# Gathered rows turned by VectorE instead of TensorE, and small transfers moved from GpSimd's queue to SyncE's, in an attention and mixture-of-depths kernel

## The chip, the core and the metric

The kernel runs on one core of a Trainium2 chip. The metric is device time in microseconds (us) of one execution; a lower time is better. Engines are named as in the profile: PE is TensorE (PEld its weight loads), DVE is VectorE, ACT is ScalarE, POOL is GpSimd, SP is SyncE, which here only issues DMA transfers.

## What is computed

Eight sequences of 448 tokens pass through sigmoid attention with 12 heads of 64, and the result is the input x (448 x 768 per sequence) of a layer that sends only 128 tokens of each sequence through a feed-forward network. Everything is float32.

```python
scores = scale * np.matmul(q, k.transpose(0, 1, 3, 2)) - np.log(S)
attn = 1.0 / (1.0 + np.exp(-scores))
x = np.matmul(attn, v)                   # then (B,H,S,D) -> (B, S, H*D)
...
scores = np.einsum('bsd,d->bs', x, w_gate)
out = x.copy()
for b in range(B):
    top_idx = np.argpartition(-scores[b], capacity)[:capacity]   # 128 of 448
    xe = x[b, top_idx]
    h = np.maximum(xe @ w1, 0.0)         # 768 -> 1024
    ye = h @ w2                          # 1024 -> 768
    g = 1.0 / (1.0 + np.exp(-scores[b, top_idx]))
    out[b, top_idx] = x[b, top_idx] + g[:, None] * ye
```

## The kernel before

**Stages and units.** Four heads of one sequence form a group; a sequence has three groups, b has groups 3b to 3b+2. A stage s (0 to 11) works on two groups, 2s and 2s+1, in seven units n = 0 to 6. `unit(s, n)` (L197) makes 32 matmuls of scores (L213) into two PSUM tiles and two sigmoids on ACT (L221). After each unit `gap(s, n)` (L471) puts other work on the queues. The second matmul, attention times v, is `values(s, n)` (L224, matmuls L248): its part 0 stands at (s, 6), its parts 1 to 3 at (s+1, 0) to (s+1, 2). "(s, n)" below means the gap after unit n of stage s. Stage 12 has gaps only; after it a tail finishes the last sequences.

**Order.** The order is written out by hand: `manual_schedule` keeps the order of the program on every engine, and each engine and each DMA queue takes its own instructions strictly in that order. Tiles come from pools; an instruction that writes a buffer of a pool waits until the last reader of its former content is done.

**PSUM.** Two score tiles ("psc") and two tiles o0 and o1, each of two banks. `values` accumulates into o0 and o1; when its part 3 is done, `take` (L257) has VectorE copy them, transposed in 32 x 32 blocks, to x_b in SBUF: four instructions at L263, the first two empty o0, the others o1. Only then can o0 take the feed-forward's first group of the stage at (s, 3).

**Choosing the tokens of sequence b**, over about three stages, s being 2, 3, 5, 6, 8, 9, 11, 12 for b = 0 to 7:

- (s, 2), (s, 3): `gate_part` (L267; L271, L274), then `gate` (L285) on VectorE sums the gate score of each token; a DMA on POOL's queue writes them to DRAM (scores, L298).
- (s, 4): `store` (L276) writes x_b to DRAM in four DMAs of 2688 rows of 128 bytes (L280, SP's queue); `spread` (L307) brings the scores back to all 128 partitions (rep, L310, POOL's queue); for b = 1 it stands at (3, 6).
- (s+1, 1): `ranking` (L450): eight VectorE operations over 448 scores (L318, L321) count for each token how many are above it; `place` (L325) writes the ranks to DRAM and reads them back to all partitions (ranks L331, spot L333, both on POOL's queue). This stands on VectorE ahead of the stage's four L263.
- (s+1, 4): `copy_out` (L282) copies x from the DRAM buffer to the output (SP's queue).
- (s+2, 0), for b = 0 at (3, 6): `choose` (L455), `select` (L338): VectorE turns ranks into 128 row numbers and gates; POOL's indirect DMA gathers those rows (xe, L361).
- (s+2, 3): `follow` (L459): `turn_rows` (L366) transposes the 128 x 768 rows by six TensorE instructions (L375) into PSUM, ACT copies them to xeT (L381), and six groups of the feed-forward are put in a list: three `ffn1` (L384; 36, 36 and 24 matmuls, L391), three `ffn2` (L396; 16 matmuls, L401, then VectorE's L403).

At (s, 3), (s, 4) and (s, 5) `go` (L423) takes one group from the list, and at (s, 5) of stages 0 to 7 a second one while the list has more than one (L481). After stage 12 the tail (L522 to L540) does the rest: the last group of sequence 4, all of 5, 6 and 7, with `choose(6)`, `ranking(7)`, `copy_out(7)` and `choose(7)` between them. After each sequence's last ffn2 (for b = 7 after every one) an indirect DMA on POOL's queue writes the finished rows to the output (L408). It waits for the copies to the output that stand before it.

**SP's queue** holds all loads: k and q of group 2s+3 at (s, 1) and of 2s+4 at (s, 5) (L95), v for stage s+1 at (s, 0) (eight DMAs, L114 and L116, which wait until `values` is done with the buffer, at the end of (s, 2)), the weights, `store` and `copy_out`.

Of the kernel before, what the change touches and what calls it, by code (L numbers as in the profile page):

```python
# [17 lines left out]
def kernel(  # L18
# [11 lines left out]
    nc = tc.nc  # L30
# [15 lines left out]
    KD = D // P  # L46
    KF = F // P
    ND = D // 3
    SLOTS = [(s, min(P, CAP - s)) for s in range(0, CAP, P)]

    NC = -(-TB // 4)
    HELD = [TT * len(range(c, TB, NC)) for c in range(NC)]
# [1 line left out]
    NEG_LOG_S = -math.log(S)  # L54
    PSUM = bass.MemoryType.PSUM
    assert Dh == 2 * TT and TB == HK + 2 and S == TT * TB and H == 4 * NG and NQ == 2 * NS
    assert D == KD * P and F == KF * P and KF % 4 == 0 and 0 < CAP < S and D == HP * P


    const = ctx.enter_context(tc.tile_pool(name="const", bufs=1))  # L60
# [76 lines left out]
    earlier = const.tile([P, NC, S], mybir.dt.uint8, name="earlier")  # L137

    number = const.tile([P, TB, TT], mybir.dt.int16, name="number")
    slots = {s0: const.tile([P, 1], F32, name=f"slot{s0}") for s0, _ in SLOTS}  # L140
    score = const.tile([P, NC], F32, name="score")
    above = const.tile([P, NC], F32, name="above")
    level = const.tile([P, NC], F32, name="level")
# [3 lines left out]
    def constants():  # L147
        make_identity(nc, iden)
        for a in range(4):
            p = slice(a * TT, (a + 1) * TT)  # L150
            nc.gpsimd.dma_start(
                out=wg_b[p],
                in_=bass.AP(tensor=moe_w_gate.tensor, offset=moe_w_gate.offset + a * TT,
                            ap=[[0, TT], [P, HP], [1, TT]]))
        for s0, slot in slots.items():
            nc.gpsimd.iota(slot, pattern=[[0, 1]], base=s0, channel_multiplier=1,
                           allow_small_or_imprecise_dtypes=True)

        nc.gpsimd.memset(above, float(S))
        nc.gpsimd.memset(level, 0.0)  # L160
        for t in (score, gate_s, place_s):
            nc.gpsimd.memset(t, 0.0)
        mine = moe.tile([P, NC], F32, name="place")
        for a in range(4):
            nc.gpsimd.iota(mine[a * TT:(a + 1) * TT], pattern=[[1, NC]], base=a * NC,
                           channel_multiplier=TB, allow_small_or_imprecise_dtypes=True)
        every = moe.tile([P, TB, TT], F32, name="rep", bufs=2)
        nc.gpsimd.iota(every, pattern=[[1, TB], [TB, TT]], base=0, channel_multiplier=0,
                       allow_small_or_imprecise_dtypes=True)
        nc.gpsimd.tensor_copy(number, every)  # L170
        for c in range(NC):
            nc.gpsimd.tensor_scalar(
                out=earlier[:, c, :], in0=every.rearrange("p r t -> p (r t)"),
                scalar1=mine[:, c:c + 1], scalar2=None, op0=ALU.is_lt)
# [107 lines left out]
    def copy_out(b):  # L282
        nc.sync.dma_start(out=out[b], in_=st[b]["x_d"])

    def gate(b):  # L285


        nc.vector.tensor_reduce(out=gate_s[:, :TB], in_=gate_parts[b], axis=AX.X, op=ALU.add)
        by_dim = moe.tile([P, TT], F32, name="by_dim")
        nc.vector.transpose(by_dim, gate_s)  # L290
        parts = moe.tile([TT, 4, TT], F32, name="parts")
        for a in range(4):
            nc.vector.tensor_copy(parts[:, a], by_dim[a * TT:(a + 1) * TT])
        total = moe.tile([TT, TT], F32, name="total")
        nc.vector.tensor_reduce(out=total, in_=parts.rearrange("p a t -> p t a"), axis=AX.X,
                                op=ALU.add)
        scores = dram.tile([TB, TT], F32, name="scores")
        nc.gpsimd.dma_start(out=scores, in_=total[:TB])  # L298
        by_token = moe.tile([TT, TT], F32, name="by_token")
        nc.vector.transpose(by_token, total)  # L300
        for m in range(4):
            n = min(NC, TB - m * NC)
            nc.vector.tensor_copy(score[m * TT:(m + 1) * TT, :n],
                                  by_token[:, m * NC:m * NC + n])
        st[b]["scores"] = scores

    def spread(b):  # L307
        scores = st[b]["scores"]
        rep = st[b]["rep"] = moe.tile([P, S], F32, name="rep", bufs=2)
        nc.gpsimd.dma_start(out=rep, in_=bass.AP(tensor=scores.tensor, offset=scores.offset,  # L310
                                                 ap=[[0, P], [1, S]]))

    def rank(b, c):
        rep = st[b]["rep"]
# [10 lines left out]
    def place(b):  # L325

        nc.vector.tensor_add(place_s[:, :NC], above, level)
        by_col = moe.tile([P, TT], F32, name="by_col")
        nc.vector.transpose(by_col, place_s)
        ranks = dram.tile([P, TT], F32, name="ranks")  # L330
        nc.gpsimd.dma_start(out=ranks, in_=by_col)  # L331
        spot = moe.tile([P, 4, NC * TT], F32, name="spot")
        nc.gpsimd.dma_start(  # L333
            out=spot, in_=bass.AP(tensor=ranks.tensor, offset=ranks.offset,
                                  ap=[[0, P], [TT * TT, 4], [1, NC * TT]]))
        st[b]["spot"] = spot.rearrange("p m c -> p (m c)")[:, :S]

    def select(b, s0, n):  # L338

        picked = []  # L340
        for what in (number.rearrange("p r t -> p (r t)"), st[b]["rep"]):
            got = moe.tile([P, 1], F32, name="got", bufs=4)
            junk = moe.tile([P, S], F32, name="scr")
            nc.vector.scalar_tensor_tensor(
                out=junk[:n], in0=st[b]["spot"][:n], scalar=slots[s0][:n], in1=what[:n],
                op0=ALU.is_equal, op1=ALU.mult, accum_out=got[:n, 0:1])
            picked.append(got)
        row = moe.tile([P, 1], I32, name="row", bufs=2)
# [14 lines left out]
            in_offset=bass.IndirectOffsetOnAxis(ap=row[:n, 0:1], axis=0))  # L363
        st[b].update(idx=idx, gate=gt, xe=xe)

    def turn_rows(b, n, where="o"):  # L366
        if b == B - 3:
            lent = attnp.tile([P, 2, S], F32, name="attn0", bufs=NU + 3)
            xeT = lent[:, :, :KD // 2 * P].rearrange("p a (k n) -> p a k n", n=P)
        else:  # L370
            xeT = moe.tile([P, 2, KD // 2, P], F32, name="xeT")
        ps = banks(where).rearrange("p a (k n) -> p a k n", n=P)
        for t in range(KD):
            a, i = divmod(t, KD // 2)
            nc.tensor.transpose(ps[:, a, i, :n], st[b]["xe"][:n, t * P:(t + 1) * P],  # L375
                                iden[:n, :n])
        if where == "any":
            nc.scalar.activation(xeT[:, 0, :, :n], ps[:, 0, :KD // 2, :n], AF.Copy)
            nc.vector.tensor_copy(xeT[:, 1, :, :n], ps[:, 1, :KD // 2, :n])
        else:  # L380
            nc.scalar.activation(xeT[:, :, :, :n], ps[:, :, :KD // 2, :n], AF.Copy)  # L381
        st[b]["xeT"] = xeT

    def ffn1(b, n, f0, f1, where):  # L384
        xeT = st[b]["xeT"]
        if f0 == 0:
            st[b]["hT"] = moe.tile([P, KF, P], F32, name="hT")
        ps = banks(where)[:, 0].rearrange("p (k n) -> p k n", n=P)
        for f in range(f0, f1):
            for t in range(KD):  # L390
                nc.tensor.matmul(ps[:, f - f0, :n], w1_sb[:, t, f * P:(f + 1) * P],  # L391
                                 xeT[:, t // (KD // 2), t % (KD // 2), :n],
                                 start=(t == 0), stop=(t == KD - 1))
        nc.scalar.activation(st[b]["hT"][:, f0:f1, :n], ps[:, :f1 - f0, :n], AF.Relu)  # L394

    def ffn2(b, n, part, where):  # L396
# [26 lines left out]
    def go(where="o"):  # L423
        if ready:
            fn, args = ready.pop(0)
            fn(*args, where)

    late = {}

    def put(where, s, n, fn, *args):  # L430
        where.setdefault((s, n), []).append((fn, args))
# [5 lines left out]
    def routed(b):  # L437

        s = (NG * b + NG - 1) // 2 + 1
        put(late, s, 4, store, b)  # L440
        put(late, s, 4 if b != 1 else 6, spread, b)
        if s == NS:
            return
        put(late, s + 1, 1, ranking, b)
        put(late, s + 1, 4, copy_out, b)
        if s + 2 <= NS:
            put(late, *((s + 1, 6) if b == 0 else (s + 2, 0)), choose, b)
            put(late, s + 2, 3, follow, b)

    def ranking(b):  # L450
        for c in range(NC):
            rank(b, c)
        place(b)

    def choose(b):  # L455
        for s0, n in SLOTS:
            select(b, s0, n)

    def follow(b, where="o"):  # L459
        for s0, n in SLOTS:  # L460
            turn_rows(b, n, where)
            routed_groups(b, n)

    def gates(i):
        gate_part(i)
# [5 lines left out]
    def gap(s, n):  # L471
# [5 lines left out]
        if 3 <= n < NU - 1:  # L477
            if not ready:
                due(late, s, n)
            go("any" if s == NS else "o")  # L480
            if n == NU - 2 and s < NS - 4 and len(ready) > 1:  # L481
                go()
        if n == NU - 1 and s < NS:
            values(s, 0)
        due(late, s, n)
        if n == 3 and s > 0:
            if waiting:
                gate(waiting.pop())
# [4 lines left out]
    def stream():  # L493
# [35 lines left out]
        copy_out(B - 1)  # L529
        while len(ready) > 1:  # L530
            go("any")
        follow(B - 2, "any")
        for n in range(2):
            go("any")
        choose(B - 1)
        while len(ready) > 1:
            go("any")
        follow(B - 1, "any")
        while ready:
            go("any")  # L540
        assert not late
# [32 lines left out]
```

## Time and profile before

| what | value |
|---|---|
| median of 3 runs (lowest, highest) | 475.2 us (473.3, 479.42) |
| the profiled execution's own time | 476.17 us |
| its span in the profile | 474.4 us |
| mean granted TensorE clock | 0.991 |
| score matmuls into psc, L213 | 2496 x 542 ns each, 153.9 us busy |
| attention times v, L248 into o | 2304 x 540 ns with raw_v, 384 x 536 ns with raw_h |
| transposes of gathered rows, L375 | 48 x about 273 ns |
| copies of them by ACT, L381 | 6 x 0.81 us |

The profile is that of one execution. The busy time of an engine is the time in which it has at least one instruction under way; matmuls overlap each other, so the mean of one is longer than its share of the time. The chain of waits follows the work that ended last backwards and so gives the pieces that follow each other without overlap. The timeline gives each engine's instructions with their start, and in brackets how long the engine stood idle before and what it waited for. "SPq" is SP's DMA queue: the duration of an issue there is the time that the issuing took, not the time of the transfer. The DMA view gives the time from an issue to its landing.

### The profile page before, as it was taken

What the parts mean: (1) busy time and instruction counts of PE and PEld (TensorE: products, weight loads), DVE (VectorE), ACT (ScalarE), POOL (GpSimd) and SP (SyncE); (2) the same over time, 40 slices, a digit from 0 to 9 for tenths busy, and PEclk for the clock granted to TensorE, in tenths of its full rate; (3) what the DMA queues carried; (4) which work ended last, traced back from release to release, by engine and by line L of the source; (5) the groups of instructions that cost most, each with busy time, mean ns of one, the idle gap of its engine ahead of it and who ended that gap; (6) DMA issues with size and microseconds to landing.
All of it is one profiled execution on the core that took longest, in us unless ns stands there. A gap on an engine that the chain in (4) does not pass through costs nothing.

```text
span 474.4 us, 14579 instructions
## 1 busy us (share of the span) xinstructions
PE 457.4 (96%) x6582; PEld 312.6 (66%) x6582; DVE 227.3 (48%) x559; ACT 184.9 (39%) x245; POOL 48.8 (10%) x76
## 2 busy tenths in 40 slices
PE   8998989897999999999999999999999999999994
PEld 3563635365765684658774666755678738999993
DVE  4309087749140825765710864946254618530100
ACT  4756464544235334435445334445344420101000
POOL 9000000110000011011100011011010010220001
PEclk9999999999899999999999999999999999999999
DMA  8988788799921980985940992985822734722000
GB/s 268 229 324 212 291 196 178 158 262 195 227 70 45 202 202 8 229 177 149 258 171 3 202 202 43 266 153 130 254 69 43 155 83 79 209 57 68 35 0 33
DMA packets 119005, 72.74 MB, mean 153 GB/s; under 512 B 96320, under 2 KB 108800, under 8 KB 118688
## 3 DMA queue, kind: packets, MB, share of 16 engines
q1 hardware_dynamic: 115808, 61.35, 50.8%
q0 software_dynamic: 3136, 10.47, 10.0%
q8 instruction: 51, 0.84, 0.7%
q14 instruction: 10, 0.08, 0.0%
HBM read 57.51 MB, written 25.31 MB: 175 GB/s over the span
## 4 chain that ended last, share of the span: by engine, by line
PE 89%; DMA 4%; DVE 2%; ACT 1%; issue 1%; SPq 0%; POOLq 0%; DVEq 0%; ACTq 0%
PE o L248 25%; PE psc L213 24%; PE o L391 16%; PE o L401 13%; PE psc L401 4%; PE psc L391 3%; PE o L213 2%; DMA raw_h<-in_v_dram 1%; ACT attn L221 1%; DMA scores<-total 1%; DMA rep<-scores 1%; PE o L375 1%; PE o L506 1%; DVE scr L321 1%; DVE scr L318 1%
## 5 line engine op out<-in xcount | busy, mean ns | idle before, releaser
L221 ACT ACTIVATE attn<-psc,bias_s 128x896 f32<-128x896 f32 x156 | 148.6, 1004 | 121.0 <-PE psc L213 120.8
L213 PE MATMUL psc<-qT,kT 32*64 32x448 f32 x2496 | 153.9, 542 | 4.2 <-ACT attn L221 4.2
L248 PE MATMUL o<-attn,raw_v 32*64 32x448 f32 x2304 | 142.2, 540 | 1.1 <-ACT o L251 1.1
L213 PEld LDWEIGHTS psc<-qT,kT 32*64 32x64 f32 x2496 | 66.4, 131 | 57.6 <-issue 33.9
L248 PEld LDWEIGHTS o<-attn,raw_v 32*64 32x64 f32 x2304 | 70.2, 133 | 46.3 <-issue 33.4
L391 PEld LDWEIGHTS o<-xeT,w_sb 128*128 128x128 f32 x576 | 67.2, 196 | 9.8 <-issue 5.7
L263 DVE STREAM_TRANSPOSE x_b<-o 128x448 f32<-128x448 f32 x48 | 26.9, 617 | 97.1 <-PE o L248 97.0
L391 PE MATMUL o<-xeT,w_sb 128*128 128x128 f32 x576 | 69.8, 281 | 0.9 <-ACT xeT L381 0.9
L401 PE MATMUL o<-w_sb,hT 128*128 128x256 f32 x272 | 62.5, 383 | 0.0
L401 PEld LDWEIGHTS o<-w_sb,hT 128*128 128x128 f32 x272 | 50.5, 190 | 14.2 <-issue 4.3
L188 DVE STREAM_TRANSPOSE kT<-raw_k 128x384 f32<-128x384 f32 x48 | 24.7, 552 | 34.2 <-PE psc L213 27.5
L403 DVE SCALAR_TENSOR_TENSOR xe<-o,gate,xe 128x256 f32<-128x256 f32 x17 | 8.2, 483 | 53.4 <-PE o L401 53.3
L318 DVE TENSOR_SCALAR_CACHE_REDUCE scr<-rep,score 128x448 f32<-128x448 f32 (+1 forms) x32 | 21.5, 673 | 20.1 <-DMA rep<-scores 19.2
L274 DVE TENSOR_REDUCE gate_p<-scr 128x14 f32<-128x448 f32 x48 | 29.8, 621 | 1.7
L271 DVE TENSOR_TENSOR scr<-x_b,wg_b 128x448 f32<-128x448 f32 x48 | 29.4, 613 | 1.1
L248 PE MATMUL o<-attn,raw_h 32*64 32x448 f32 x384 | 28.8, 536 | 0.0
L394 ACT ACTIVATE hT<-o 128x384 f32<-128x384 f32 (+1 forms) x20 | 9.1, 453 | 49.5 <-PE o L391 49.5
L401 PE MATMUL psc<-w_sb,hT 128*128 128x256 f32 x112 | 25.4, 380 | 0.0
L195 DVE STREAM_TRANSPOSE qT<-raw_q 128x896 f32<-128x896 f32 x23 | 24.7, 1073 | 1.4 <-DMA raw_q<-in_q_dram 1.4
L401 PEld LDWEIGHTS psc<-w_sb,hT 128*128 128x128 f32 x112 | 21.0, 190 | 3.4 <-issue 0.7
L321 DVE SCALAR_TENSOR_TENSOR scr<-rep,score,earlier 128x448 f32<-128x448 f32 (+1 forms) x32 | 21.8, 683 | 1.4
L298 POOL DMA_DIRECT2D scores<-total x8 | 4.4, 555 | 173.5 <-DVE by_token L300 165.3
(69 smaller groups left out, 222.7 us busy)
## 6 DMA issues: line engine op xcount, KB each, us to landing
raw_k<-in_k_dram SPq DMA_DIRECT2D x24, 448.0 KB, 5.1
raw_q<-in_q_dram SPq DMA_DIRECT2D x24, 448.0 KB, 4.7
x_d<-x_b SPq DMA_DIRECT2D x32, 336.0 KB, 7.6
out_dram<-x_d SPq DMA_DIRECT2D x8, 1344.0 KB, 8.5
raw_v<-in_v_dram SPq DMA_DIRECT2D x48, 192.0 KB, 4.4
w_sb<-in_moe_w_dram SPq DMA_DIRECT2D x6, 512.0 KB, 5.7
w_sb<-in_moe_w_dram SPq DMA_DIRECT2D x8, 384.0 KB, 9.0
spot<-ranks POOLq DMA_DIRECT2D x8, 256.0 KB, 6.2
```

Source lines behind the costliest of these rows:

```text
L188: nc.vector.transpose(kT[i][:, e, :HK], sk[:, e, :HK].rearrange("p (m c) d -> p c m d", c=NF))
L195: nc.vector.transpose(qT[i], sq)
L213: nc.tensor.matmul(psc[h // 2][y * Dh:(y + 1) * Dh, h % 2, :S], kT[2 * s + x][d, e, r:r + 2, :].rearrange("d r t -> d (r t)"), qT[2 * s + ...
L221: nc.scalar.activation(a, psc[pr][:, :, :S], AF.Sigmoid, bias=bias_s, scale=QK_SCALE)
L248: nc.tensor.matmul(o[x][j * Dh:(j + 1) * Dh, pr, :S], w, a[rows, j, :], start=(n == 0 and c == 0), stop=(n == 3 and c == NF - 1))
L263: nc.vector.transpose(x_tiles[b][:, :, 2 * g + pr, :], outs[s][x][:, pr, :S].rearrange("p (r t) -> p r t", t=TT))
L271: nc.vector.tensor_tensor(out=tmp, in0=x_tiles[b][:, :, hp, :], in1=wg_b[:, hp:hp + 1, :].to_broadcast([P, TB, TT]), op=ALU.mult)
L274: nc.vector.tensor_reduce(out=gate_parts[b][:, :, hp], in_=tmp, axis=AX.X, op=ALU.add)
L318: nc.vector.tensor_scalar(out=junk[:n], in0=rep[:n], scalar1=own, scalar2=0.0, op0=ALU.is_gt, op1=ALU.add, accum_out=above[:n, c:c + 1])
L321: nc.vector.scalar_tensor_tensor(out=junk[:n], in0=rep[:n], scalar=own, in1=earlier[:n, c, :], op0=ALU.is_equal, op1=ALU.mult, accum_out=l ...
L391: nc.tensor.matmul(ps[:, f - f0, :n], w1_sb[:, t, f * P:(f + 1) * P], xeT[:, t // (KD // 2), t % (KD // 2), :n], start=(t == 0), stop=(t = ...
L401: nc.tensor.matmul(ps[:n, :ND], st[b]["hT"][:, t, :n], w2_sb[:, t, cols], start=(t == 0), stop=(t == KF - 1))
```

## The change

In sequences 0 to 5 the gathered rows are turned by VectorE: `turn_blocks` transposes 32 x 32 blocks, 16 instructions of 32 partitions x 192 elements, each from one quadrant of the partitions to another, straight from SBUF to SBUF; TensorE's six transposes and ACT's copy are gone there. Sequences 6 and 7 in the tail keep TensorE's way. For sequences 2 to 7 the four small transfers (scores, rep, ranks, spot) are issued on SP's queue instead of POOL's, at the same places of the program. `store` of sequence 1 moves from (3, 4) to (4, 1), ahead of its `ranking`. `choose` moves to (s+1, 6) for all; `turn_blocks` stands at (4, 1) for b = 0, ahead of `ranking(1)` on VectorE, and at (s+2, 4) for the others; the groups of b go on the list at (s+2, 3) for b = 0 and at (s+2, 5) for the others. The second group at (s, 5) is taken in stages 7, 8 and 9 only. The loop over slots of 128, which had one turn, is gone, and the line numbers shift by a few.

```diff
+    def queue(b):
+        return nc.gpsimd if b < 2 else nc.sync
...
-        nc.gpsimd.dma_start(out=scores, in_=total[:TB])
+        queue(b).dma_start(out=scores, in_=total[:TB])
...
-        nc.gpsimd.dma_start(out=rep, in_=bass.AP(tensor=scores.tensor, offset=scores.offset,
-                                                 ap=[[0, P], [1, S]]))
+        queue(b).dma_start(out=rep, in_=bass.AP(tensor=scores.tensor, offset=scores.offset,
+                                                ap=[[0, P], [1, S]]))
...
-        nc.gpsimd.dma_start(out=ranks, in_=by_col)
+        queue(b).dma_start(out=ranks, in_=by_col)
...
-        nc.gpsimd.dma_start(
+        queue(b).dma_start(
             out=spot, in_=bass.AP(tensor=ranks.tensor, offset=ranks.offset,
                                   ap=[[0, P], [TT * TT, 4], [1, NC * TT]]))
...
-    def turn_rows(b, n, where="o"):
+    def turn_blocks(b, n):
+        xeT = turned(b)
+        xe = st[b]["xe"].rearrange("p (k m d) -> p m k d", m=4, d=TT)
+        for m in range(4):
+            for s0 in range(0, n, TT):
+                nc.vector.transpose(xeT[m * TT:(m + 1) * TT, :, s0:s0 + TT],
+                                    xe[s0:s0 + TT, m])
+
+    def turn_rows(b, n):
...
         s = (NG * b + NG - 1) // 2 + 1
-        put(late, s, 4, store, b)
-        put(late, s, 4 if b != 1 else 6, spread, b)
+        put(late, *((s + 1, 1) if b == 1 else (s, 4)), store, b)
+        put(late, s, 6 if b == 1 else 4, spread, b)
         if s == NS:
             return
+        if b == 0:
+            put(late, s + 2, 1, turn_blocks, b, CAP)
         put(late, s + 1, 1, ranking, b)
         put(late, s + 1, 4, copy_out, b)
         if s + 2 <= NS:
-            put(late, *((s + 1, 6) if b == 0 else (s + 2, 0)), choose, b)
-            put(late, s + 2, 3, follow, b)
+            put(late, s + 1, 6, choose, b)
+            if b > 0:
+                put(late, s + 2, 4, turn_blocks, b, CAP)
+            put(late, s + 2, 3 if b == 0 else 5, routed_groups, b, CAP)
...
+    FOURTH = (7, 8, 9)
...
-            if n == NU - 2 and s < NS - 4 and len(ready) > 1:
-                go()
         if n == NU - 1 and s < NS:
             values(s, 0)
         due(late, s, n)
+        if n == NU - 2 and s in FOURTH:
+            go()
```

## The prediction, made before the changed kernel ran

> **What bounds the kernel now.** I read the page's busy times first, then the chain of waits, then the timelines of the queues around the edits.
>
> ```profile
> PE 457.4 (96%) x6582; PEld 312.6 (66%) x6582; DVE 227.3 (48%) x559; ACT 184.9 (39%) x245; POOL 48.8 (10%) x76
> ...
> PE 89%; DMA 4%; DVE 2%; ACT 1%; issue 1%; SPq 0%; POOLq 0%; DVEq 0%; ACTq 0%
> ```
>
> TensorE is busy 96% of the span and carries 89% of the chain. So a TensorE instruction removed is time gained, and anything that makes TensorE wait is time lost, however idle the others are. The chain in order of time, at stages 5 to 7:
>
> ```profile
> 191.50 1.53 PE psc L213 x32
> ...
> 223.57 1.50 PE psc L213 x32
> 225.08 3.68 PE o L401 x16
> 228.75 0.66 PE o L375 x6
> ```
>
> The pieces join without a gap; a turn of gathered rows costs the chain 0.66 us, no more, because a unit of scores (1.69) follows it and covers ACT's copy. Only at sequence 0 it stands bare:
>
> ```profile
> 113.60 1.19 DVE x_b L263 x2
> 114.79 0.25 issue
> 115.04 0.86 PE o L375 x6
> 115.92 0.82 ACT xeT L381
> ```
>
> There TensorE waits for o0 to be emptied (L263), because ranking(1) held VectorE until 113.5; the first ffn1 starts at 116.78.
>
> **Part 1, turns off TensorE.** Sequences 1 to 5: 5 x 0.66 = 3.3 us off the chain. ACT's six copies (0.81 each) lie beside other work: nothing.
>
> **Part 2, the turns on VectorE.** Each sequence gets 16 transposes of 32 partitions x 192 elements.
>
> ```profile
> L188 DVE STREAM_TRANSPOSE kT<-raw_k 128x384 f32<-128x384 f32 x48 | 24.7, 552 | 34.2 <-PE psc L213 27.5 <-PE o L213 3.5 <-DMA raw_k<-in_k_dram 3.1
> L190 DVE STREAM_TRANSPOSE kT<-raw_k 128x128 f32<-128x128 f32 x24 | 6.5, 269 | 0.0
> ```
>
> Between 269 (128 elements) and 552 (384) 192 lies at 340 ns, about 310 in a row: 16 x 0.31 = 5.0 us. Bounds: 16 x 0.18 = 2.9 (the small copies L293, four in 0.72 us) and 16 x 0.55 = 8.8. VectorE is idle half the time, so only three places matter.
> - Sequence 0: turn_blocks(0) now stands ahead of ranking(1). The gather is issued at 98.87 and lands 5.2 us later, 104.1; +5.0 = 109.1; ranking takes 6.2 (107.33 to 113.55); two L263 1.2: o0 free at 116.6, against the first ffn1 at 116.78 now. With store(1) gone from there the gather may land a us earlier. I take a gain of 0.7; bounds: loss 3.7 (8.8 for the turns), gain 3.9 (o0 free at 112.8, when TensorE is there).
> - Stage 7: the extra ffn1(2) at (7, 5) comes 1.69 + 3.65 = 5.3 us after the ffn2 whose VectorE step (0.48) precedes the 16 turns: 5.5 against 5.3, loss 0.2; bounds 0 and 4.0.
> - Elsewhere a whole stage of other groups lies between the turns and their ffn1: nothing; if the cover went, 5 us each.
>
> [...] The trace has TensorE's turn at 0.66 us on the engine that makes the chain, and VectorE idle for half the span, so 5.0 us there are the cheaper ones. [...]
>
> **Part 3, the small transfers on SP's queue.** This is what decides. Before, for sequence 3, SP and POOL:
>
> ```profile
> 197.63 0.53 SPq L283 DMA_DIRECT2D out_dram<-x_d  x1
> 198.36 13.89 SPq L280 DMA_DIRECT2D x_d<-x_b  x4
> 212.35 3.85 SPq L95 DMA_DIRECT2D raw_k<-in_k_dram  x1
> ```
> ```profile
> 201.00 0.54 POOL L298 DMA_DIRECT2D scores<-total  x1 [12.28 <-DVE by_token L300]
> 207.01 0.56 POOL L310 DMA_DIRECT2D rep<-scores  x1 [5.47 <-DMA scores<-total]
> ```
> ```profile
> raw_k<-in_k_dram SPq DMA_DIRECT2D x1, 448.0 KB, 7.2
> ```
>
> The four store DMAs take 13.89 us to issue, and the load behind them takes 3.85 to issue instead of 0.38 and lands 7.2 later (median 5.1): a transfer behind a store on this queue lands 212.35 + 7.2 - 198.36 = 21.2 us after the store's first issue. The same sum is 20.2 at sequence 1 (94.49; 108.61 + 6.1), both with a copy_out just ahead, and 16.7 at sequence 0 without one (65.63; 76.32 + 6.0). POOL's rep passes by: 4.6 us from issue to landing. In the changed order rep stands behind the store, and the store behind scores, which waits for VectorE's sum. rep has half the bytes of raw_k, so I take 1 us less: 15.7 alone, 19.7 behind a copy_out. Behind the waiting rep, VectorE's ranking (6.2) and then L263 are queued, and TensorE's first group at (s+1, 3) waits for o0.
>
> Now each sequence, with t0 = the end of TensorE's values part 3 at (s, 2):
> - b = 3: t0 = 191.5. SP issues v, k and q until 5.8 as before, then ranks(2), which lands behind those loads (last issue 196.91 + median 4.7 = t0 + 10.1) at 10.6; spot(2) until 11.5; scores(3), ready since 9.2 (200.70), until 12.1; copy_out(2) until 12.8; store(3); rep lands at 12.8 + 19.7 = 32.5; ranking to 38.8; o0 free at 40.0. TensorE comes to (7, 3) after 4 units (1.69), three ffn1 (4.2, 4.2, 2.9) and values (3.0, 3.0, 2.25, 2.25 with four units of 1.5), 34.6. **Wait 5.4 us**; bounds 0 (rep as on POOL) and 7.4 (21.2, and ranks as slow as the 5.7 of sequence 1).
> - b = 5: t0 = 294.35; the same steps with scores ready at 9.2 give store(5) at 13.0, rep at 32.7, o0 at 40.2. TensorE's three groups of stage 9 gain an ffn2 (3.65): now 34.5, then 38.2. **Wait 2.0**; bounds 0 and 4.5.
> - b = 2, 4, 6: no copy_out between; store at t0 + 7.2 to 7.9, rep at 23 to 24, o0 at 31 or before, against 34.0, 38 and (L263 of sequence 6 after values) 30.9: nothing, but sequence 2 and 6 have only 2 to 3 us.
> - b = 7, the tail. Scores(7) is ready at 401.7. copy_out(6), now issued at 376.87, and store(7), now at 394.68, stand behind it: store at 403.1, rep at 403.1 + 15.7 to 19.7; I take 421.5, ranking to 427.7. VectorE has the ffn2 steps of sequence 5 and its half of xeT(6) queued behind:
>
> ```profile
> 420.42 0.66 PE psc L375 x6
> 421.08 3.46 PE o L401 x16
> 424.54 4.02 PE psc L391 x36
> ```
> ```profile
> 415.84 0.21 DVE L329 STREAM_TRANSPOSE by_col<-place_s 128x32 f32<-128x32 f32 x1
> ```
>
>   Ranking ends at 416.05 now, and ffn1(6) starts at 424.54; then xeT(6) is ready at 427.7 + 2 x 0.4 + 0.56 = 429.1, a wait of 4.6. After it ranks, spot, copy_out(7) (issue about 431, 8.5 to land), the output of sequence 5 that waits for that copy, and the gather of xe(7) into its buffer follow one another, to about 448.7, against the turn at 442.16 + 4.6. **Wait in all 5.5** (between 4.6 and 6.5); bounds 0 and 9.
>
> POOL's queue loses 24 issues of 0.53 to 0.77 us; no one waits for them. Store(1) at (4, 1) stands behind the loads of v(5), which wait for values until 111; its gather is not due before about 131, copy_out(1) then holds SP until about 134, and the next load (now 138.3) is not late: nothing.
>
> [...]
>
> **Sum.** 3.3 + 0.7 gained; 0.2 + 5.4 + 2.0 + 5.5 = 13.1 lost. Net +9.1 on the profiled execution's 476.17 (span 474.4 and 1.8 around it): **485.3 us**. The median before is 475.2, so this is 2.1% over it; about 2% (9.5 us) is also what a measurement of this kernel tells from no change.
>
> **Rivals.**
> - *The turns leave, the transfers stay hidden.* If rep overtakes the stores or the stores drain faster, only parts 1 and 2 remain: 476.2 - 3.8 = 472.4, faster than before. It decides when rep lands by t0 + 27 in stage 6 (34.6 - 7.4) and by about 417 in the tail. For: POOL's row. Against: three raw_k rows.
> - *Only the tail waits.* Stages 6 and 9 have slack because the stores there drain as quickly as the tail's (9.0 us to issue): 472.4 + 5.5 = 477.9.
> - *VectorE becomes late.* Transposes across quadrants cost 0.55: sequence 0 loses 3.7 instead of gaining 0.7, stage 7 loses 4.0: 485.3 + 4.4 + 3.8 = 493.5. For: no row shows such a shape. Against: L190's 269.
>
> **How the numbers follow.** Main case 0.57, own range 480 to 491 (half of its chance beyond 484.7); hidden 0.18; only the tail 0.12; VectorE late 0.13. Slower by over 2%: 0.28 + 0.13 = 0.41. Faster by over 2% would need 465.7, more than all the turns and the wait at sequence 0 are worth (3.3 + 3.9): 0.03 of the hidden case. Within 2%: 0.29 + 0.12 + 0.15 = 0.56. The range for 8 in 10 runs from the hidden case, 472, to 493, about the late one.
>
> **What would show it.** Right: PE waiting for L263 at the first group of stage 7 by about 5 us and stage 10 by 2, VectorE's L318 waiting for rep at sequences 3, 5 and 7, a gap of some 5 us before ffn1(6). Wrong: rep landing within 10 us of the store's first issue; L263 not waited for; transposes far from 310 ns each.

## The result, and the profile after

| | before | after |
|---|---|---|
| median (lowest, highest) | 475.06 us (473.3, 479.42) | 495.83 us (494.85, 499.2) |
| the profiled execution, and its span | 476.17, 474.4 | 495.78, 494.0 |
| mean granted TensorE clock | 0.991 | 0.975 |

The ratio is 1.0435, 95% interval 1.035 to 1.0521: 4% slower, where 485.3 us (2.1%) with a range of 472 to 493 had been predicted. Both kernels were timed four times here; the median ahead of the prediction is that of three. Line numbers of the changed kernel: scores L211, values L246, the emptying of o0 and o1 L261, ffn1 L405, ffn2 L414 with VectorE's L416, VectorE's turns L385, ranking L320 and L323, the transfer of the gate scores L300, copy_out L281, rep L312, store L278.

The page of the changed kernel, its span, its busy times and its chain by engine:

```profile
span 494.0 us, 14572 instructions
...
PE 457.9 (93%) x6546; PEld 298.9 (61%) x6546; DVE 262.5 (53%) x655; ACT 180.3 (37%) x239; POOL 33.6 (7%) x52
...
PE 66%; SPq 11%; DVE 10%; DMA 9%; ACT 2%; issue 2%; POOLq 0%; DVEq 0%; ACTq 0%
```

TensorE's busy time is as before (457.4), though six turns are gone; its idle time, span less busy, has gone from 17.0 to 36.1 us. The chain now runs over SP's queue, DMA and VectorE for 30%, where it had 6%. What VectorE and TensorE waited for, in the waits view (engine, tile and line, what was waited for: us in total, times, longest):

```profile
DVE scr L320 <- DMA rep<-scores: 51.0, 6, 17.8
...
PE o L414 <- DVE x_b L261: 11.1, 2, 6.8
...
PE o L405 <- DVE x_b L261: 6.4, 1, 6.4
...
PE psc L405 <- DVE xe L416: 4.9, 1, 4.9
```

The second row holds stage 7 (6.75) and stage 10 (4.33), the third is sequence 0, the fourth the tail. The places are those of the prediction. SP's timeline at sequence 3 shows the cause: scores, copy_out(2), the store, and rep behind it:

```profile
193.05 0.45 SPq L300 DMA_DIRECT2D scores<-total  x1
193.59 0.53 SPq L281 DMA_DIRECT2D out_dram<-x_d  x1
194.17 15.94 SPq L278 DMA_DIRECT2D x_d<-x_b  x4
210.22 2.76 SPq L312 DMA_DIRECT2D rep<-scores  x1
```

VectorE can start its ranking at 217.23, 23.1 us after the store's first issue. The chain carries the same thing at stage 10 (start, us):

```profile
327.06 7.49 DMA rep<-scores
334.67 0.70 DVE scr L320 x2
...
340.79 1.17 DVE x_b L261 x2
342.09 5.38 PE o L414 x16
```

rep, the eight operations of the ranking, the emptying of o0, and then TensorE, in one unbroken line. The last row holds what the prediction has no word for. The same 16 matmuls take 3.67 us where TensorE comes to them without a wait (232.66, 349.16). TensorE's granted clock (PEclk, as a share of its full speed) over the three groups that follow a long wait (stretch; its length, busy times, then PEclk, DMA share, GB/s), after:

```profile
224.65:230.97 6.32, 6.32 (x24) 4.86 (x26) 3.30 (x6) 0.00 (x0) 0.00 (x0) 0.58 0.30 87
...
342.09:347.47 5.38, 5.38 (x24) 4.18 (x27) 3.29 (x6) 0.00 (x0) 0.00 (x0) 0.68 0.57 183
442.90:449.79 6.89, 6.89 (x38) 6.89 (x39) 1.10 (x3) 0.00 (x0) 0.00 (x0) 0.60 0.43 121
```

and two of the corresponding groups before, and the one after the wait that the old kernel had at sequence 0:

```profile
116.78:122.69 5.91, 5.91 (x44) 5.79 (x46) 3.96 (x7) 0.00 (x0) 0.76 (x1) 0.71 1.23 354
225.08:228.76 3.68, 3.68 (x18) 3.22 (x19) 3.27 (x6) 1.90 (x2) 0.00 (x0) 1.00 0.89 138
...
424.54:428.56 4.02, 4.02 (x38) 4.02 (x38) 1.97 (x8) 0.00 (x0) 1.19 (x1) 1.00 0.23 98
```

These three waits are thus paid twice: once as idle time, then as a group at 0.58 to 0.68 of the clock. The three groups take 6.32, 5.38 and 6.89 instead of 3.67, 3.67 and 4.02: 7.2 us. The two traces, step by step:

| where | us |
|---|---|
| five turns gone from TensorE, 0.66 each | -3.3 |
| first ffn1(0): starts at 117.06, was 116.78 | +0.3 |
| wait at stage 7's first group | +6.75 |
| wait of the extra ffn1(2) at (7, 5) for L385 | +1.26 |
| wait at stage 10's first group | +4.33 |
| wait before ffn1(6) in the tail | +4.90 |
| lower clock after these three long waits | +7.2 |
| from TensorE's last instruction to the end: 5.2, was 7.0 | -1.8 |
| sum | +19.6 |

The spans differ by 19.6 too. Why the end is shorter was not followed up.

### The profile page after: what moved, and what is told of

It is laid out like the page before. It is cut to its first block, busy times and chain, and to the rows that moved or that the text cites. A ratio compares the mean times of both kernels' runs of the same rounds, so it can differ in the third digit from the quotient of the medians.

```text
span 494.0 us, 14572 instructions
## 1 busy us (share of the span) xinstructions
PE 457.9 (93%) x6546; PEld 298.9 (61%) x6546; DVE 262.5 (53%) x655; ACT 180.3 (37%) x239; POOL 33.6 (7%) x52
## 4 chain that ended last, share of the span: by engine, by line
PE 66%; SPq 11%; DVE 10%; DMA 9%; ACT 2%; issue 2%; POOLq 0%; DVEq 0%; ACTq 0%
PE o L246 22%; PE psc L211 18%; PE o L405 9%; SPq L278 9%; PE o L414 8%; DVE xeT L385 4%; DMA rep<-scores 3%; PE psc L405 3%; PE o L211 3%; PE psc L414 2%; ACT attn L219 2%; DMA ranks<-by_col 2%; DMA raw_h<-in_v_dram 1%; DMA raw_q<-in_q_dram 1%; DVE x_b L261 1%
## 5 line engine op out<-in xcount | busy, mean ns | idle before, releaser
L211 PE MATMUL psc<-qT,kT 32*64 32x448 f32 x2496 | 145.9, 540 | 4.2 <-ACT attn L219 4.2
L246 PE MATMUL o<-attn,raw_v 32*64 32x448 f32 x2304 | 131.8, 535 | 1.5 <-ACT o L249 1.1
L211 PEld LDWEIGHTS psc<-qT,kT 32*64 32x64 f32 x2496 | 59.1, 131 | 62.6 <-issue 42.0
L246 PEld LDWEIGHTS o<-attn,raw_v 32*64 32x64 f32 x2304 | 60.0, 132 | 53.0 <-issue 43.3
L405 PEld LDWEIGHTS o<-xeT,w_sb 128*128 128x128 f32 x576 | 67.4, 196 | 17.5 <-issue 10.8
L405 PE MATMUL o<-xeT,w_sb 128*128 128x128 f32 x576 | 70.2, 282 | 7.7 <-DVE x_b L261 6.4
L414 PE MATMUL o<-w_sb,hT 128*128 128x256 f32 x272 | 66.7, 402 | 11.1 <-DVE x_b L261 11.1
L414 PEld LDWEIGHTS o<-w_sb,hT 128*128 128x128 f32 x272 | 53.7, 201 | 26.6 <-issue 16.9
L261 DVE STREAM_TRANSPOSE x_b<-o 128x448 f32<-128x448 f32 x48 | 26.9, 617 | 76.7 <-PE o L246 76.7
L320 DVE TENSOR_SCALAR_CACHE_REDUCE scr<-rep,score 128x448 f32<-128x448 f32 (+1 forms) x32 | 21.6, 676 | 51.9 <-DMA rep<-scores 51.0
L385 DVE STREAM_TRANSPOSE xeT<-xe 32x192 f32<-32x192 f32 x80 | 29.5, 369 | 4.3 <-DMA xe<-x_d,row 3.1
L421 POOL DMA_INDIRECT out_dram<-xe,idx x10 | 10.0, 997 | 282.1 <-DVE xe L416 143.2
L246 PE MATMUL o<-attn,raw_h 32*64 32x448 f32 x384 | 26.4, 535 | 0.0
L414 PE MATMUL psc<-w_sb,hT 128*128 128x256 f32 x112 | 25.4, 380 | 0.0
L414 PEld LDWEIGHTS psc<-w_sb,hT 128*128 128x128 f32 x112 | 21.0, 190 | 3.4 <-issue 0.7
L323 DVE SCALAR_TENSOR_TENSOR scr<-rep,score,earlier 128x448 f32<-128x448 f32 (+1 forms) x32 | 21.8, 682 | 1.4
```

The lines of the kernel that those rows point to most:

```text
L211: nc.tensor.matmul(psc[h // 2][y * Dh:(y + 1) * Dh, h % 2, :S], kT[2 * s + x][d, e, r:r + 2, :].rearrange("d r t -> d (r t)"), qT[2 * s + ...
L246: nc.tensor.matmul(o[x][j * Dh:(j + 1) * Dh, pr, :S], w, a[rows, j, :], start=(n == 0 and c == 0), stop=(n == 3 and c == NF - 1))
L261: nc.vector.transpose(x_tiles[b][:, :, 2 * g + pr, :], outs[s][x][:, pr, :S].rearrange("p (r t) -> p r t", t=TT))
L385: nc.vector.transpose(xeT[m * TT:(m + 1) * TT, :, s0:s0 + TT], xe[s0:s0 + TT, m])
L414: nc.tensor.matmul(ps[:n, :ND], st[b]["hT"][:, t, :n], w2_sb[:, t, cols], start=(t == 0), stop=(t == KF - 1))
```

## The experiments

Two theories stood against each other. *The queue*: the loss comes from rep standing behind the store on SP's queue, by the waits and the low clock after them. *VectorE*: the loss comes from VectorE, which now has 16 turns per sequence more and is late for the emptying of o0. Each ratio below is against the kernel before, run on the same chip, with its 95% interval; "us" are medians.

**All small transfers on POOL's queue** (the changed kernel otherwise):

```diff
-        return nc.gpsimd if b < 2 else nc.sync
+        return nc.gpsimd
```

> The changed kernel with one edit undone: scores, rep, ranks and spot of all sequences on POOL's queue again; VectorE's turns, their places and the later store(1) stay. Theory (rep behind the store on SP's queue makes TensorE wait, and after each wait the granted clock is half for some us): the waits before stage 7 (6.75 us), stage 10 (4.33) and ffn1(6) (4.90) go, and with them the slow matmuls behind them (2.6, 1.7 and 2.8); 495.8 - 23.1 = 473, and the wait of 6.4 at sequence 0 stays. Rival (the 16 turns on VectorE and their places cost the time): no transfer decides, 485 or more.

Measured: 477.8 us, ratio 1.0002 (0.9966 to 1.0038). All three waits and the low clock behind them are gone; what remains of the change's waits is 6.7 at sequence 0 and 1.3 at (7, 5). So the 4% goes with the queue; what is left of the change comes to nothing in sum, within 0.4% either way. That the turns win nothing here is a question for the last experiments.

**The kernel before, with nothing but the transfers of sequences 2 to 7 on SP's queue** (the same line in all four places):

```diff
+    def queue(b):
+        return nc.gpsimd if b < 2 else nc.sync
...
-        nc.gpsimd.dma_start(out=rep, in_=bass.AP(tensor=scores.tensor, offset=scores.offset,
+        queue(b).dma_start(out=rep, in_=bass.AP(tensor=scores.tensor, offset=scores.offset,
```

> The kernel before with only the transfers of sequences 2 to 7 moved to SP's queue; the turns stay on TensorE. Theory: the same waits appear without any turn on VectorE, at stage 7 6 us, at stage 10 5 to 6 (its groups are one ffn2 shorter than in the changed kernel), in the tail 5, each followed by 2 to 3 us of half clock: 476 + 24 = 500, at least 492. Rival (the turns cost the time): about 476.

Measured: 497.54 us, ratio 1.0438 (1.0361 to 1.0515), the same loss as that of the whole change without one turn on VectorE. It waits 7.62 us at stage 7, 6.48 at stage 10 and 3.17 before ffn1(6). Its PE timeline at stage 7:

```profile
232.18 5.07 PE L405 MATMUL o<-w_sb,hT 128*128 128x256 f32 x16 [7.62 <-DVE x_b L263]
```

The VectorE theory falls as the cause of the loss.

**rep ahead of the store** (the changed kernel, sequences 2 to 7):

```diff
+        if b >= 2:
+            put(late, s, 4, spread, b)
         put(late, *((s + 1, 1) if b == 1 else (s, 4)), store, b)
-        put(late, s, 6 if b == 1 else 4, spread, b)
+        if b < 2:
+            put(late, s, 6 if b == 1 else 4, spread, b)
```

> The changed kernel with rep of sequences 2 to 7 issued ahead of the store on the same SP queue instead of behind it; all else as in the changed kernel. Theory: it is the place behind the store, not SP's queue as such; rep lands some 10 us earlier, the three waits and their half clock go, while each store starts 2 to 3 us later (SP waits for scores to land): 474, between 472 and 479. Rival (SP's queue as such is slower for small transfers, or SP blocked by the waits for scores and ranks delays the loads): most of the loss stays, 485 or more.

Measured: 476.11 us, ratio 0.9943 (0.9906 to 0.998). SP's timeline at sequence 3, and VectorE's first operation of the ranking:

```profile
201.62 0.33 SPq L312 DMA_DIRECT2D rep<-scores  x1
202.00 10.89 SPq L278 DMA_DIRECT2D x_d<-x_b  x4
```
```profile
206.71 0.68 DVE L320 TENSOR_SCALAR_CACHE_REDUCE scr<-rep,score 128x448 f32<-128x448 f32 x1 [1.12 <-DMA rep<-scores]
```

The same transfer on the same queue is issued in 0.33 us and there after 5.1. It is not SP's queue that costs, it is the place in it. Nor is it the store's traffic as such: in the kernel before, POOL's rep was issued in the middle of the same store (207.01, the store from 198.36 to 212.25), and its median landing was 4.6. The waits at stages 7 and 10 are gone; sequence 0's (4.7), (7, 5)'s (1.3) and 2.6 in the tail, where the gather of xe(6) is late, are left.

**Only rep on SP's queue** (scores, ranks and spot back on POOL's):

```diff
-        queue(b).dma_start(out=scores, in_=total[:TB])
+        nc.gpsimd.dma_start(out=scores, in_=total[:TB])
```

> The changed kernel with only rep of sequences 2 to 7 on SP's queue; scores, ranks and spot are on POOL's again. Chain theory (it takes both: scores, behind ranks and spot, hold the store back on SP by 4 us in the loop and 21 in the tail, and rep stands behind the store): without the first, rep lands about 20 us after a store that starts at t0 + 6.9, o0 is free at t0 + 34.5 against TensorE's 34.6 at stage 7 and 38.2 at stage 10, and in the tail rep lands at about 410: 477, at most 480. Simple theory (the place behind the store alone costs it): the waits at stages 7 and 10 stay at 3 us or more and draw the half clock, 484 or more.

Measured: 485.09 us, ratio 1.0161 (1.0093 to 1.0229): the time is that of the simple theory, the wait at stage 10 of neither. TensorE waits 3.27 at stage 7 and 1.75 at stage 10, not at all in the tail; at sequence 3 rep is there 21.1 us after the store's first issue (195.94 to 217.05). rep's place behind the store alone makes these waits. The other three transfers on SP's queue add the rest, 3.5 and 2.6 and the whole of the tail's. A later start of the store is only part of that: without them the store goes out 1.7 us earlier in stage 6 (9.1 after t0, with t0 as in the prediction, against 10.8), but 0.6 later in stage 9, and rep takes 2.0 and 3.3 us less behind it. Why it takes less was not followed up.

**TensorE kept busy in two of the waits.** The changed kernel, with six added matmuls of 512 columns ahead of stage 7's first group and three ahead of stage 10's; nothing reads their results.

```diff
+    FILL = {(7, 3): 6, (10, 3): 3}
...
+            if (s, n) in FILL:
+                warm = banks("psc")
+                for _ in range(FILL[s, n]):
+                    nc.tensor.matmul(warm[:, 0], w1_sb[:, 0, :P], w1_sb[:, 0, :512],
+                                     start=True, stop=True)
```

> The changed kernel with extra matmuls whose result nobody reads (each 128x512, about 0.85 us at full clock) in the waits before stage 7 (six) and stage 10 (three); the waits themselves stay as long. Theory (TensorE's idle time of several us drops its granted clock to half for 3.4 or 6.8 us after it, which cost 2.6 us behind the first wait and 1.7 behind the second): the clock stays full there and the time falls by 4.3, to 491.5 (489 to 493). Rival (the half clock does not come from the idle time, or what is lost in it is hidden): 495.8 as before, or more by what the extra matmuls push back.

Measured: 492.84 us, ratio 1.0342 (1.0293 to 1.0392), against 1.0435 without them: 0.93% of the time before or 4.4 us less, with more work on TensorE (the six took 5.27 us, 223.73 to 229.00, that is 0.88 each). The two groups had been 2.65 and 1.71 us longer than elsewhere, 4.4 together. That the two figures agree so well is partly chance: the two intervals overlap, and in the profiled execution other waits differ as well (7.87 at sequence 0 instead of 6.42). What decides is the clock. The windows view of this kernel over stage 7's added matmuls and most of the first group after them, and that group in the timeline:

```profile
223.73:229.15 5.42, 5.42 (x13) 2.35 (x14) 5.18 (x17) 0.84 (x1) 0.00 (x0) 1.00 1.12 239
229.00:232.30 3.30, 3.30 (x16) 2.94 (x16) 3.20 (x6) 0.00 (x0) 0.00 (x0) 1.00 0.33 113
```
```profile
229.00 3.72 PE L414 MATMUL o<-w_sb,hT 128*128 128x256 f32 x16
```

The clock stays at 1.00, and the group takes 3.72 us instead of 6.32; stage 10's takes 3.62 instead of 5.38. So the lower clock behind these two waits is a result of TensorE's idle time, and a cost of its own.

**Sequence 0 turned by TensorE again** (the changed kernel otherwise, its transfers on SP's queue):

```diff
-        if b == 0:
-            put(late, s + 2, 1, turn_blocks, b, CAP)
...
                 put(late, s + 2, 4, turn_blocks, b, CAP)
+            else:
+                put(late, s + 2, 3, turn_rows, b, CAP, "o")
```

> The changed kernel with only sequence 0's rows turned by TensorE at (4, 3) again; the transfers stay on SP's queue. Theory: of the 19.6 us only the wait at sequence 0 goes, 6.4 to about 2.5 with one 3.4 us spell of half clock less: 495.8 - 4 = 492, ratio 1.035; the waits at stages 7, 10 and in the tail stay as they are. Rival (the wait at sequence 0 starts the later ones): all waits shrink, 485 or less.

Measured: 492.73 us, ratio 1.0307 (1.0253 to 1.0361). The wait at sequence 0 falls to 1.8, 0.6 and 0.7. The others did not stay as they were in the profiled execution: 8.60 at stage 7, 3.79 at stage 10, 0.84 and 3.05 in the tail, where the changed kernel had 6.75, 4.33 and 4.90. Between this and the whole change the intervals overlap, so the size of this part, about 1%, is not secured.

**The turns without the transfers:** all transfers on POOL's queue, sequence 0 as above, and turn_blocks(2) one gap earlier, which takes the wait of 1.26 at (7, 5) away. The later store(1), the earlier `choose` and the new order of the groups stay.

```diff
-                put(late, s + 2, 4, turn_blocks, b, CAP)
+                put(late, s + 2, 3 if b == 2 else 4, turn_blocks, b, CAP)
```

> The turns alone, without the transfers: all small transfers on POOL's queue, sequence 0's rows turned by TensorE at (4, 3), sequences 1 to 5 on VectorE, sequence 2's at (7, 3); store(1) later as in the changed kernel. Theory: with no wait added the gain is the five turns, 3.3 us, on the time before: 472 (470.5 to 473.5), ratio 0.993. Rival (VectorE's 6.1 us per sequence delay something else, or the earlier gain came from rep on SP): 475, ratio 1.0.

Measured: 475.95 us, ratio 0.9965 (0.9931 to 0.9999): 1.7 us won (0 to 3.3), half of the 3.3 that left TensorE. In the profiled execution sequence 0 waited 2.98, 0.58 and 0.73 us where the kernel before had 2.2 and 0.9, and the mean granted clock was 0.983 where it was 0.991. There the whole gain is gone: this execution is the slowest of its twelve, 1.3 us longer than the profiled one of the kernel before. So what takes back half in the median is not shown.

**Store(1) later, in the kernel before:**

```diff
-        put(late, s, 4, store, b)
+        put(late, *((s + 1, 1) if b == 1 else (s, 4)), store, b)
```

> The kernel before with only store of sequence 1 moved from (3, 4) to (4, 1). Theory: rep(1) no longer shares the DMA engines with the store, lands 3 us or more earlier, VectorE's ranking(1) ends before TensorE needs o0, and the wait of 2.2 us and up to 3.4 us of lost clock go: 475 - 4 = 471 (469 to 473). Rival (the transfer is hidden anyway, the wait comes from VectorE's own work): 475.

Measured: 475.41 us, ratio 0.996 (0.9913 to 1.0007). A miss: rep(1) does land faster, 3.3 us after its issue instead of 5.2, but POOL issues it later (104.40 against 101.99), and the ranking starts at 107.81 where it started at 107.33. What this part is worth cannot be told from nothing; nor, its ratio being that of the run before, how much of that run's 1.7 us is its own.

**copy_out one gap earlier,** with rep ahead of the store:

```diff
-        put(late, s + 1, 4, copy_out, b)
+        put(late, s + 1, 3, copy_out, b)
```

> Rep ahead of the store as in the run before, and only copy_out moved to (s+1, 3). Theory: the output of sequence 4 no longer waits for copy_out(6), so xe(6) comes earlier and the 2.6 us before its turn go, and the DMA engines are free of the copy when rep is read: 473. Rival: another wait (o0 or xeT) takes its place, 476.

Measured: 475.69 us, ratio 0.9993 (0.996 to 1.0026). The 2.6 us in the tail are gone, but sequence 0 waited 7.6 in the profiled execution. Inconclusive: it can't be told from the kernel with rep ahead alone (0.9943).

**All that helped, together:** rep ahead of the store, copy_out earlier, sequence 0 turned by TensorE, turn_blocks(2) one gap earlier (the edits above).

> Rep ahead of the store as in the run before, and: sequence 0's rows turned by TensorE at (4, 3) again, sequence 2's turns on VectorE at (7, 3) instead of (7, 4), copy_out at (s+1, 3), ahead of the next sequence's scores on SP. Theory: the wait of 4.7 us at sequence 0 and its clock, 1.3 at stage 7 and 2.6 before the turn of sequence 6 go, and what stays is the gain of the turns: 476 - 7 = 469 (466 to 472), faster than both kernels. Rival (TensorE waits for rep(1) at sequence 0 in any case, and copy_out ahead of rep delays it): 473 to 476.

Measured: 473.24 us, ratio 0.9943 (0.9905 to 0.9981). It is 0.6% faster than the kernel before, and so faster than both, but no faster than rep ahead of the store alone, which had the same ratio. The gain is less than half of the 6 to 7 us expected. The profiled execution, the fastest of the ten, has 1.4 and 0.6 us at sequence 0 and no other of the new waits. In it TensorE takes 347.5 us from its first ffn1(0) to its last matmul (115.02 to 462.50), against 350.6 in the kernel before (116.78 to 467.35), with the first 36 matmuls of ffn1(0) slower than the next 36 in each, by 1.9 us (6.18, in two pieces, against 4.29) and 1.7 (5.91 against 4.21). There the five turns' 3.3 us do show.

## Why the prediction was wrong

The direction and the places of the three large waits were right: VectorE waits for rep, TensorE for VectorE, where the prediction said. The sum was 9.1 where the trace has 19.6.

- **The step that failed is the pricing of the waits, "Wait 5.4 us", "Wait 2.0", "Wait in all 5.5": each as idle time only.** The sum has no term for the granted clock after a wait. It measured 2.65, 1.71 and 2.87, in all 7.2 us, and in the first two places the added matmuls showed that it is caused by the idleness. With these 7.2 us, known only afterwards, the sum would have stood at 492.5; the mis-sized terms below, and the end that was 1.8 shorter, make up the rest. The trace before had shown the effect, in its chain:

```profile
116.78 5.91 PE o L391 x36
...
124.39 4.21 PE o L391 x36
```

  The same 36 matmuls, the first time after waits of 2.2 and 0.9 us: 1.7 us more. I had the row of that wait before me and read on to the next wait.
- **rep behind the store, mis-sized.** "rep lands at 12.8 + 19.7 = 32.5" after t0 was 33.8 in stage 6 (t0 = 183.40, rep 217.23). Two errors partly cancelled: the store went out at 10.8, not 12.8, but rep took 23.1 behind it, not 19.7. In stage 9 it was 34.9 instead of 32.7 (22.9 behind the store). Hence 6.75 and 4.33 for 5.4 and 2.0; TensorE's arrival was right within 0.3 us both times. The guess that half the bytes make rep 1 us faster than raw_k had the wrong sign: raw_k's own 21.2 would have been nearer. In the tail it was 20.0 for the 15.7 to 19.7 given.
- **The tail** waited 4.90 before ffn1(6), predicted 4.6 and 0.9 more after it, which did not come. The way differed a little: the prediction let TensorE wait for xeT(6), but the wait ended once L416, queued on VectorE behind the late ranking, had emptied the PSUM tile (442.75); VectorE's half of xeT(6) came after that.
- **The turns on VectorE, mis-sized.** 369 ns each, 6.1 us per sequence, against 310 and 5.0. That moves sequence 0 from a gain of 0.7 to a loss of 0.3, and (7, 5) from 0.2 to 1.26: some 2 us. The row:

```profile
L385 DVE STREAM_TRANSPOSE xeT<-xe 32x192 f32<-32x192 f32 x80 | 29.5, 369 | 4.3 <-DMA xe<-x_d,row 3.1
```

- **"Sequences 1 to 5: 5 x 0.66 = 3.3 us off the chain"** is not refuted: with the transfers back on POOL's queue 1.7 us were won, and the interval (nothing to 3.3) leaves the size open. The trace of the last experiment has 3.1 us less on TensorE after sequence 0. VectorE's time elsewhere made no wait on TensorE, as said.
- **"b = 2, 4, 6: nothing"** held: VectorE's late ranking there made no wait on TensorE.
- **The rivals.** "The transfers stay hidden" is refuted for this order, and comes true when rep goes ahead of the store. "VectorE becomes late" would have given about the right time (493.5) by the wrong cause: with the queue undone the turns cost nothing in sum.

That the 5.0 us on VectorE "are the cheaper ones" is not refuted: the run with the turns and without the transfers is, if anything, faster (0.9931 to 0.9999), for a kernel whose VectorE is idle half the time (busy 48% of the span before the change); how much of that is the turns' is open.

## What to carry to other kernels

A small transfer that an engine waits for belongs ahead of a large one on the same queue, or on another queue; what counted here was what stood ahead of it (at sequence 3 rep was there 5.1 us after its issue ahead of the store, and 23.1 us after the store's first issue behind it), not which queue it was on (4.6 in the median on POOL's in the kernel before). When a wait on the bounding engine is priced, price the work after it as well (7.2 us here): look in the same trace for that work once after a wait and once in a row. And an engine idle half of the time is free only where no one waits for what stands behind the new work on it (at sequence 0 the first ffn1 came 0.3 us later here, though TensorE's own turn was gone).

## What the runs showed of the hardware

- **The clock fell to half in steps of 3.4 us, on a grid of its own.** In the profiled executions of the kernel before and of the changed kernel it was 1.0 or 0.5, and the stretches at 0.5 that ended inside the span lasted 3.4 or 6.8 us. In the changed kernel they begin at 113.92, 223.15, 342.62 and 441.60, that is 32, 35 and 29 steps of 3.413 us apart; in the kernel before at 93.71 and 117.60, 7 steps apart. The waits of 6.75 and 4.90 brought 6.8 us of it, of which 5.3 and 5.5 lay behind the wait; that of 4.33 brought 3.4, all behind it. The groups were longer by about half of that (2.65, 2.87 and 1.71). Behind a wait of 3.27 (only rep on SP's queue) a group of 16 matmuls took 6.64 us instead of 3.67; behind one of 2.60 (rep ahead, tail) and one of 1.75 (only rep, stage 10) such a group of 16 took 3.62 and 3.69, as in a row. But one of 1.40 in the kernel before (90.55 to 91.95) brought 3.4 us at half clock, from 93.71 on. The length of the wait alone does not set it.
- **A store of four DMAs of 2688 rows of 128 bytes held its queue.** Its issues took 15.9 us right behind a copy_out at sequence 3 and 10.9 with rep in between; the issue of rep behind the store took 2.4 to 4.1 us instead of 0.33 ahead of it at sequence 3, and rep was there 20 to 23 us after the store's first issue at sequences 3, 5 and 7.
- **Transposes of 32 x 192 float32 from quadrant to quadrant** took 369 ns each on VectorE, in each of the nine kernels in which they ran.
